# A fused linear attention and gated MLP on one core: more column groups of the first layer by the seven-product scheme, with v casts, sums and gates on GpSimd

## The chip, the core and the metric

The kernel runs on one core of one Trainium2 chip. The metric is device time in microseconds (us) of one execution, lower is better. Four compute engines matter here: TensorE (PE, with its weight loads shown apart as PEld), VectorE (DVE), ScalarE (ACT) and GpSimd (POOL). SyncE (SP) and GpSimd issue the DMAs. Each engine works off its own queue in order; semaphores tie the queues together.

## The reference

The inputs are q, k and v of 8 batches, 8 heads, 576 positions and 64 columns, and two weight matrices, 512 x 2048 and 2048 x 512. All are float32, and so is the output of 4608 x 512.

```python
q_p = concat(relu(q) * cos_w, relu(q) * sin_w)      # features, 128 wide
k_p = concat(relu(k) * cos_w, relu(k) * sin_w)
kv  = einsum('bhsf,bhsd->bhfd', k_p, v);  z = k_p.sum(axis=2)
x   = einsum('bhsf,bhfd->bhsd', q_p, kv) / (einsum('bhsf,bhf->bhs', q_p, z) + 1e-6)
h   = x.transpose(0, 2, 1, 3).reshape(4608, 512) @ w_in     # first layer
out = (h * cos(h)) @ w_out                                  # gate, second layer
```

## The kernel before

The 4608 tokens are cut into nine chunks of 512. Chunks 0 to 7 are the first 512 tokens of one batch each; chunk 8 collects the 64 left over of every batch. For each batch `attention` loads k, v and q by SP, makes the features with `prep` (ReLU times cosine or sine, float32 to float16, L419 on ACT or L420 on DVE, 128x512 each), casts v with `cast_v` (L433 ACT, L434 DVE), forms kv in `kv` (L446), transposes the q features by DMA in `q_dma` (L485) or on PE in `q_pe` (L475), and forms the numerator and denominator in `num` (L507 PE, L523 to L527 DVE). The normalised x is transposed on PE (`x_pe`, L547 and L551) for chunks up to 2 and by DMA (`x_dma`, L557) after that. Features of k and q lie in one tile `KQ`, with five slots of one token block each for k and five for q.

The first layer is in `layer1`. Chunks 0 and 1 run it on halves of the tokens (L604). From chunk 2 on, the 16 column tiles of h form four groups: group g holds tiles 2g and 2g+1 of the lower half and the same of the upper half. A group can be done in two ways.

- `layer1_plain` (L636): four banks, each four products of 128x512, 16 in all. Each bank then has a cosine on ACT (`gate`, L577) and a product on DVE (L579) that writes float16 into gT.
- `layer1_fast` (L740): the two by two block product by seven half-size products (Winograd's form), so 28 matmuls of 128x256. It needs four sums of weights (`w_in_sums`, L676) and four differences of x (`layer1_sums`, L697). Its products are gathered in three float32 tiles Y, U and Z by three copies on ACT (L748) and three additions on DVE (L752). Y gets a gate of its own (cosine L577, product L579), U and Z share a cosine of 1024 columns (L763) and a product of 1024 columns (L769), and the last part is gated straight out of PSUM.

Before, groups 0 and 1 of chunks 3 to 8 take the fast way, 12 groups; the others of chunks 2 to 8, 16 groups, the plain way. The sums of w_in cover two groups at once, 1024 columns each.

The second layer (`layer2`, L897) is by seven products from chunk 1 on, with sums of gT on DVE (L879, L924), copies on ACT (L908) and additions on DVE (L912). Stores of the output leave through POOL's queue (L803).

The order of the work is written out by a planner, `Plan`, when the kernel is built. Every step is added with an engine or a choice of engines, an occupation, a latency, a due time and the keys it reads and writes. `forward` simulates the engines with those costs, `run` repeats it over perturbed priorities (`ROUNDS`) and keeps the plan that ends first, and the instructions are then emitted in that order. Steps with `port=True` may not run on DVE and POOL at the same time in the plan. In the plan of before, POOL has no arithmetic beyond a few one-row casts that order DMAs (L970, L980, L995, L1002).

Of the kernel before, what the change touches and what calls it, by code (L numbers as in the profile page):

```python
# [17 lines left out]
class Plan:  # L18
# [11 lines left out]
    PASSES, ROUNDS = 12, 117  # L30
# [3 lines left out]
    BUSY = 2.2  # L34

# [6 lines left out]
    def add(self, eng, occ, lat, due, fn, rd=(), wr=(), dma=None, lane=None, late=0.0,  # L42
            lazy=None, port=False):
# [18 lines left out]
        for key in wr:  # L62
# [6 lines left out]
                               lazy=lazy, port=port))  # L69
# [40 lines left out]
    def forward(self, key):  # L110
# [14 lines left out]
        held, other = {"DVE": 0.0, "POOL": 0.0}, {"DVE": "POOL", "POOL": "DVE"}  # L125

        def shared(n, e):
            return st[n]["port"] and e in other

        def at(n, e):  # L130
            t = max(free[e], avail[n])
            return max(t, held[other[e]]) if shared(n, e) else t
# [5 lines left out]
        def first(n, e, t):  # L138
            opts = st[n]["opts"]
            return len(opts) == 1 or all(  # L140
                t + opts[e][1] <= max(free[x], avail[n]) + o[1] for x, o in opts.items())
# [12 lines left out]
        while todo:  # L154
# [44 lines left out]
            if shared(n, e):  # L199
                held[e] = free[e]  # L200
# [60 lines left out]
def kernel(  # L261
# [57 lines left out]
    KQ = sb("KQ", [P, 2, (NT + 1) * H * 2 * D])  # L319
    kp, qp = [KQ[:, n].rearrange("p (t h g d) -> p t h g d", t=NT + 1, h=H, g=2) for n in range(2)]  # L320
# [12 lines left out]
    G2.append(KQ[:, :, 0:JH * SM].rearrange("p h (j s) -> p h j s", j=JH))  # L333
# [21 lines left out]
    VCAST = ("DVE", "ACT")  # L355
# [3 lines left out]
    GATE1 = (w_in_sb[0:2, 0, Dff // 2 + 1:Dff // 2 + 2], [("w_in", 2)])  # L359
# [11 lines left out]
    def dve(occ, due, fn, rd, wr, lat=0.13, lazy=None, port=False):  # L371
        pl.add("DVE", occ, occ + lat, due, fn, rd, wr, lazy=lazy, port=port)
# [4 lines left out]
    def either(due, cost, fn, rd, wr):  # L377

        lat = {"DVE": 0.13, "ACT": 0.15, "POOL": 0.15}
        pl.add([(e, cost[e], cost[e] + lat[e], fn[e]) for e in cost], 0, 0, due, None, rd, wr, port=True)  # L380
# [29 lines left out]
    def prep(b, nm, t, g, eng, due, hs=slice(0, H), after=()):  # L410
        dst = (kp if nm == "k" else qp)
        out_, in_ = dst[:, t, hs, g, :], raw[nm][:, hs, t, :]
# [3 lines left out]
        wr = [(nm + "p", t, g, h) for h in heads]  # L416
# [7 lines left out]
    def cast_v(b, t, eng, due, hs=slice(0, H), nt=1):  # L424
# [7 lines left out]
        cost = {"DVE": 0.09 + 0.33 * f, "ACT": 0.12 + 0.5 * f, "POOL": 0.9}  # L432
# [36 lines left out]
    def q_pe(b, t, bank, key, eng, due):  # L469
# [3 lines left out]
        def mm():  # L473
            for h in range(H):
                nc.tensor.matmul(ps[:, h, :], lhsT=qp[:, t, h].rearrange("p g d -> p (g d)"),  # L475
                                 rhs=IDENT, is_transpose=True)
        pe(H, MMT, due, mm, [("qp", t, g, h) for g in range(2) for h in range(H)] + ["ID"], [key])
# [5 lines left out]
    def q_dma(b, t, due):  # L483
        dst, dkey = qdst(b, t)
        pl.add("SP", 1.25, 0, due, lambda: nc.sync.dma_start(  # L485
            out=dst, in_=qp[:, t].rearrange("p h g d -> p (h g d)"), transpose=True),
            [("qp", t, g, h) for g in range(2) for h in range(H)], [dkey],
# [76 lines left out]
    def mul(due, cost, fn, rd, wr, pool):  # L564

        if pool is None:
            dve(cost, due, lambda: fn(nc.vector), rd, wr)
        elif pool:
            pl.add("POOL", 3.4 * cost, 0.15 + 3.4 * cost, due, lambda: fn(nc.gpsimd), rd, wr,
                   port=True)  # L570
        else:
            dve(cost, due, lambda: fn(nc.vector), rd, wr, port=True)

    def gate(bank, key, dst, dkeys, due, pool=None, rd=()):
# [9 lines left out]
    def layer1(c):  # L584
# [3 lines left out]
        if c < 2:  # L588
            n = 0
            for quarter in range(4):  # L590
                for hf in range(2):
                    for jp in range(2):
# [15 lines left out]
                        pe(2 * NCT, MMH, due, mm, xk[2 * hf:2 * hf + 2] + [("w_in", quarter)],  # L608
# [21 lines left out]
    def layer1_plain(c, j, X, xk):  # L630
# [7 lines left out]
        pe(NCT, MM, due, mm, xk + [("w_in", j // 4)], [mk])  # L638
# [4 lines left out]
    FAST1 = {3: 2, 4: 2, 5: 2, 6: 2, 7: 2, 8: 2}  # L643
    SUMS_AT = min(FAST1) - 1
    Y_POOL, UZ_POOL = (), ()
    CH2, JF = NCT // 2, JH * P // 2


    WSA = {1: w_in_sb[:, 0:CH2, 2 * JF:3 * JF]}
    for n in (2, 3, 4):  # L650
        WSA[n] = sb(f"WS{n}", [P, CH2, JF])
    LATE = any(nf > 2 for nf in FAST1.values())

    def flat(t, dt=F16):
# [3 lines left out]
    WSB = {n: qT[n - 1].rearrange("p h s -> p (h s)").rearrange("p (c f) -> p c f", c=CH2)  # L658
           for n in range(1, 5)}
# [9 lines left out]
    def w_in_sums(f, due):  # L669
        W, JL = w_in_sb, JH * P  # L670
        lo, hi = slice(f * JF, (f + 1) * JF), slice(JL + f * JF, JL + (f + 1) * JF)
        a11, a12, a21, a22 = W[:, 0:CH2, lo], W[:, CH2:, lo], W[:, 0:CH2, hi], W[:, CH2:, hi]
        ws = WSB if f else WSA

        def tt(n, a, b, op, rd, wr):
            dve(0.61, due, lambda: nc.vector.tensor_tensor(out=ws[n], in0=a, in1=b, op=op),  # L676
                [("w_in", f), ("w_in", 2 + f)] + rd, wr + [("WS", n, f)] + ([("qT", n - 1)] if f else []), lazy=20.0, port=True)
        tt(3, a11, a21, ALU.subtract, [], [])
        tt(1, a21, a22, ALU.add, [], [] if f else [("w_in", 2)])
        tt(2, ws[1], a11, ALU.subtract, [("WS", 1, f)], [])  # L680
        tt(4, a12, ws[2], ALU.subtract, [("WS", 2, f)], [])
# [7 lines left out]
    def layer1_sums(c, X, xk):  # L689
# [6 lines left out]
        def tt(n, a, b, rd, wr=()):  # L696
            dve(0.33, start[c] - 1 + 0.3 * n, lambda: nc.vector.tensor_tensor(  # L697
                out=XS[n], in0=a, in1=b, op=ALU.subtract), xk + rd, [("XS", i, n)] + list(wr), port=True)
# [9 lines left out]
    def layer1_fast(c, g, X, xk):  # L708
# [14 lines left out]
        def lhs(n):  # L723
            if n > 0:
                return (lambda cc, j: (WSB if g // 2 else WSA)[n][:, cc, (2 * (g % 2) + j) * P:
# [373 lines left out]
    for c in range(2, NC):  # L1099
        if c < B:  # L1100
            attention(c)
        if c == SUMS_AT + 1:
            w_in_sums(0, start[c] - 12)
# [40 lines left out]
```

## Time and profile before

| what | value |
|---|---|
| device time, median of 3 runs | 285.42 us (284.47 to 286.86) |
| span of the profiled execution (its own time is given only as this span) | 282.8 us |
| PE busy | 272.4 us, 96% |
| PEld busy | 208.3 us, 74% |
| DVE busy | 247.5 us, 88% |
| ACT busy | 215.5 us, 76% |
| POOL busy | 26.0 us, 9% |
| plain groups, L636: 256 matmuls of 128x512, mean of one | 379 ns |
| fast groups, L740: matmuls of 128x256, mean of one | 272 to 273 ns |
| product of a gate, L579 on DVE, 128x512, mean of one | 683 ns |
| cosine of a gate, L577 on ACT, 128x512, mean of one | 595 ns |
| product of U and Z, L769 on DVE, 128x1024, mean of one | 1217 ns |

A mean is the time from start to end of one instruction. Instructions of one engine overlap at their edges, so a row of equal ones advances faster than its mean: eight matmuls of 128x512 advance by 1.73 us, and gates on DVE by 0.60 us each. The groups of the page give the busy time, the mean of one instruction, and the idle time of the engine ahead of it. The chain of work is followed back from the last instruction to whatever released each step.

### The profile page before, as it was taken

What the parts mean: (1) busy time and instruction counts of PE and PEld (TensorE: products, weight loads), DVE (VectorE), ACT (ScalarE), POOL (GpSimd) and SP (SyncE); (2) the same over time, 40 slices, a digit from 0 to 9 for tenths busy, and PEclk for the clock granted to TensorE, in tenths of its full rate; (3) what the DMA queues carried; (4) which work ended last, traced back from release to release, by engine and by line L of the source; (5) the groups of instructions that cost most, each with busy time, mean ns of one, the idle gap of its engine ahead of it and who ended that gap; (6) DMA issues with size and microseconds to landing.
All of it is one profiled execution on the core that took longest, in us unless ns stands there. A gap on an engine that the chain in (4) does not pass through costs nothing.

```text
span 282.8 us, 6578 instructions
## 1 busy us (share of the span) xinstructions
PE 272.4 (96%) x2619; PEld 208.3 (74%) x2619; DVE 247.5 (88%) x458; ACT 215.5 (76%) x367; POOL 26.0 (9%) x53
## 2 busy tenths in 40 slices
PE   7889989999999999999999999999999999999993
PEld 2468856669866688777877887787777877876882
DVE  2986878999999999999999999999899999967941
ACT  2947897999999999999999999995834666456420
POOL 1412020011000020002000200020002001100200
PEclk9999999999999999999999999999999999999999
DMA  6999999799989999999997899786024001100124
GB/s 214 303 204 273 258 310 300 251 270 212 344 222 240 228 227 362 170 245 224 254 268 186 265 290 224 164 159 167 2 56 168 21 2 75 76 2 0 68 82 150
DMA packets 77567, 53.30 MB, mean 188 GB/s; under 512 B 46048, under 2 KB 75232, under 8 KB 77536
## 3 DMA queue, kind: packets, MB, share of 16 engines
q1 hardware_dynamic: 70032, 39.73, 55.7%
q0 software_dynamic: 6784, 12.59, 17.1%
q10 hardware_dynamic: 720, 0.57, 0.6%
q8 instruction: 20, 0.33, 0.5%
q14 instruction: 11, 0.09, 0.1%
HBM read 36.74 MB, written 9.44 MB: 163 GB/s over the span
## 4 chain that ended last, share of the span: by engine, by line
PE 84%; DMA 8%; ACT 3%; DVE 2%; issue 1%; SPq 0%; ACTq 0%; DVEq 0%
PE M L897 33%; PE M L636 16%; PE M L740 8%; PE M L604 8%; PE TR L740 4%; PE M L834 4%; DMA vm<-in_v_dram 4%; PE TR L636 3%; PE ATT L507 3%; DMA qT<-KQ 3%; PE ATT L446 3%; DMA qm<-in_q_dram 2%; ACT KQ L419 1%; PE M L475 1%; DVE x L527 1%
## 5 line engine op out<-in xcount | busy, mean ns | idle before, releaser
L577 ACT ACTIVATE ch<-M 128x512 f32<-128x512 f32 x90 | 52.8, 595 | 11.1 <-PE M L604 4.1
L897 PEld LDWEIGHTS <-gT 128*128 128x128 f16 x560 | 53.7, 98 | 9.3
L579 DVE TENSOR_TENSOR gT<-M,ch 128x512 f16<-128x512 f32 x83 | 55.4, 683 | 4.7 <-ACT ch L577 4.2
L897 PE MATMUL M<-w_out_sb,gT 128*128 128x256 f16 x448 | 54.9, 273 | 0.0
L636 PE MATMUL M<-xT,w_in_sb 128*128 128x512 f16 x184 | 45.9, 379 | 0.0
L419 ACT ACTIVATE KQ<-qm,CS 128x512 f16<-128x512 f32 x59 | 40.1, 718 | 4.5 <-DMA qm<-in_q_dram 4.5
L419 ACT ACTIVATE KQ<-km,CS 128x512 f16<-128x512 f32 x56 | 38.3, 719 | 0.0
L636 PEld LDWEIGHTS <-w_in_sb 128*128 128x128 f16 x256 | 24.4, 98 | 18.3
L803 POOL DMA_DIRECT2D out_dram<-ost x32 | 17.0, 537 | 213.9 <-DVE ost L912 134.8
L897 PE MATMUL M<-T,S 128*128 128x256 f16 x256 | 32.5, 273 | 0.0
L604 PE MATMUL M<-xT,w_in_sb 128*128 128x256 f16 x256 | 30.6, 273 | 0.1
L897 PEld LDWEIGHTS <-S 128*128 128x128 f16 x256 | 24.9, 98 | 4.0
L604 PEld LDWEIGHTS <-w_in_sb 128*128 128x128 f16 x256 | 24.5, 98 | 3.9 <-issue 0.3
L908 ACT ACTIVATE ost<-M 128x512 f32<-128x512 f32 x31 | 18.5, 597 | 10.2 <-PE M L897 10.1
L527 DVE TENSOR_TENSOR x<-ATT,rec 128x512 f16<-128x512 f32 x32 | 22.1, 691 | 1.1
L740 PEld LDWEIGHTS <-w_in_sb 128*128 128x128 f16 x192 | 18.5, 98 | 4.9 <-issue 0.2
L912 DVE TENSOR_TENSOR ost<-M,ost 128x512 f32<-128x512 f32 x24 | 16.4, 681 | 4.0 <-issue 3.5
L507 PEld LDWEIGHTS <-qT 128*128 128x128 f16 x320 | 15.1, 98 | 4.7 <-issue 0.5
L752 DVE TENSOR_TENSOR Z<-M,Z 128x512 f32<-128x512 f32 x23 | 15.6, 684 | 2.3 <-PE M L740 1.9
L879 DVE TENSOR_TENSOR S<-gT 128x2048 f16<-128x2048 f16 (+1 forms) x16 | 17.3, 1085 | 0.2
L748 ACT ACTIVATE Z<-M 128x512 f32<-128x512 f32 x19 | 11.3, 596 | 6.6 <-PE M L740 6.4
L740 PEld LDWEIGHTS <-WS 128*128 128x128 f16 x144 | 13.6, 98 | 3.3 <-issue 0.2
(130 smaller groups left out, 421.8 us busy)
## 6 DMA issues: line engine op xcount, KB each, us to landing
out_dram<-ost POOLq DMA_DIRECT2D x32, 256.0 KB, 4.3
qm<-in_q_dram SPq DMA_DIRECT2D x8, 640.0 KB, 5.8
km<-in_k_dram SPq DMA_DIRECT2D x8, 640.0 KB, 7.8
qm<-in_q_dram SPq DMA_DIRECT2D x8, 512.0 KB, 5.6
km<-in_k_dram SPq DMA_DIRECT2D x8, 512.0 KB, 6.7
vm<-in_v_dram SPq DMA_DIRECT2D x6, 640.0 KB, 6.4
vm<-in_v_dram SPq DMA_DIRECT2D x6, 512.0 KB, 5.9
w_in_sb<-in_moe_w_in_dram POOLq DMA_DIRECT2D x4, 512.0 KB, 8.9
```

The costliest lines, as they stand in the source:

```text
L419: fn = {"ACT": lambda: nc.scalar.activation(out=out_, in_=in_, func=AF.Relu, scale=sc), "DVE": lambda: nc.vector.tensor_scalar(out=out_, i ...
L507: nc.tensor.matmul(bank[hb][:, hh * D1:(hh + 1) * D1], lhsT=a[:, h, :], rhs=z[:, h, :], start=(i == 0), stop=(i == len(parts) - 1))
L527: nc.vector.tensor_tensor(out=split(x16[n][:, hs, :], k), in0=A[:, :, :, 0:D], in1=split(rec[n][:, hs], k).unsqueeze(3).broadcast_to((P, k ...
L577: act(0.5, due, lambda: nc.scalar.activation(out=ch[c], in_=bank, func=AF.Sin, bias=math.pi / 2.0, scale=1.0), [key], [("ch", c)])
L579: mul(due, 0.61, lambda q: q.tensor_tensor(out=dst, in0=bank if len(dst.shape) == 2 else bank.rearrange("p (j s) -> p j s", j=dst.shape[1] ...
L604: nc.tensor.matmul(M1[m][:, jj * 2 * P:(jj + 1) * 2 * P], lhsT=w_in_sb[:, cc, j * P:(j + 1) * P], rhs=X[:, cc, ts], start=(cc == 0), stop= ...
L636: nc.tensor.matmul(M, lhsT=w_in_sb[:, cc, j * P:(j + 1) * P], rhs=X[:, cc, :], start=(cc == 0), stop=(cc == NCT - 1))
L740: nc.tensor.matmul(bank[0][:, j * TH:(j + 1) * TH], lhsT=a(cc, j), rhs=b[:, cc, :], start=(first and j == 0 and cc == 0), stop=(last and j ...
L803: pl.add(eng, 0.9 if eng == "POOL" else 0.65, 0, due, lambda: q.dma_start(out=dst, in_=src_), keys, [], dma=(nb, 355.0))
L879: dve(0.07 + 1.07 / NG, due, lambda: nc.vector.tensor_tensor(out=out_[:, sl], in0=a[:, sl], in1=b[:, sl], op=op), rd, wr, port=True)
L897: nc.tensor.matmul(bank[0][:, tt * MH:(tt + 1) * MH], lhsT=a[:, j, tt * P:(tt + 1) * P], rhs=b[:, j, :], start=(first and tt == 0 and j == 0),
L908: act(0.5, due, lambda: nc.scalar.activation(out=dst, in_=view(bank), func=AF.Copy), [bank[1]], dk)
```

## The change

- `FAST1` sends 2 groups of chunk 2, 3 groups of chunks 3 to 6 and 4 groups of chunks 7 and 8 through the seven products, 22 groups in place of 12.
- The sums of w_in are made per group (512 columns), each when the first chunk needs it; group 3 writes into tiles of qT that are free by then. The keys of w_in are finer to match.
- v casts from chunk 2 on go to POOL (`VCAST`). The gate of Y goes to POOL (`Y_ON`). The product of U and Z and the differences of x may go to DVE or POOL as the planner finds (`UZ_ON`, `XS_ON`); in the plan that comes out 4 of 22 and 21 of 28 go to POOL.
- The planner's exclusion of DVE and POOL (`port`) is gone, POOL's costs are lower, a small preference for POOL is added, and `ROUNDS` is 200.
- q features have three slots in `KQ` in place of five.

```diff
-    PASSES, ROUNDS = 12, 117
+    PASSES, ROUNDS = 12, 200
+    RATHER = {"POOL": -0.5}
...
-            return max(t, held[other[e]]) if shared(n, e) else t
+            return max(free[e], avail[n])
...
-                t + opts[e][1] <= max(free[x], avail[n]) + o[1] for x, o in opts.items())
+                t + opts[e][1] + self.RATHER.get(e, 0.0)
+                <= at(n, x) + o[1] + self.RATHER.get(x, 0.0) + 1e-9 for x, o in opts.items())
...
-    KQ = sb("KQ", [P, 2, (NT + 1) * H * 2 * D])
-    kp, qp = [KQ[:, n].rearrange("p (t h g d) -> p t h g d", t=NT + 1, h=H, g=2) for n in range(2)]
+    NQ = 3
+    KQ = sb("KQ", [P, (NT + 1 + NQ) * H * 2 * D])
+    KQ6 = KQ.rearrange("p (t h g d) -> p t h g d", t=NT + 1 + NQ, h=H, g=2)
+    kp, qp = KQ6[:, 0:NT + 1], KQ6[:, NT + 1:]
...
-    VCAST = ("DVE", "ACT")
+    VCAST = ("POOL",)
...
-        out_, in_ = dst[:, t, hs, g, :], raw[nm][:, hs, t, :]
+        slot = t if nm == "k" else t % NQ
+        out_, in_ = dst[:, slot, hs, g, :], raw[nm][:, hs, t, :]
...
-        cost = {"DVE": 0.09 + 0.33 * f, "ACT": 0.12 + 0.5 * f, "POOL": 0.9}
+        cost = {"DVE": 0.09 + 0.33 * f, "ACT": 0.12 + 0.5 * f, "POOL": 0.2 + 0.45 * f}
...
-    def mul(due, cost, fn, rd, wr, pool):
-        if pool is None:
-            dve(cost, due, lambda: fn(nc.vector), rd, wr)
-        elif pool:
-            pl.add("POOL", 3.4 * cost, 0.15 + 3.4 * cost, due, lambda: fn(nc.gpsimd), rd, wr,
-                   port=True)
-        else:
-            dve(cost, due, lambda: fn(nc.vector), rd, wr, port=True)
+    def mul(due, cost, fn, rd, wr, on=""):
+        slow = 2.15 * cost
+        opts = {"DVE": ("DVE", cost, cost + 0.13, lambda: fn(nc.vector)),
+                "POOL": ("POOL", slow, slow + 0.15, lambda: fn(nc.gpsimd))}
+        pl.add([opts[e] for e in ("DVE", "POOL") if e[0] in (on or "D")], 0, 0, due, None, rd, wr)
...
-    FAST1 = {3: 2, 4: 2, 5: 2, 6: 2, 7: 2, 8: 2}
-    SUMS_AT = min(FAST1) - 1
-    Y_POOL, UZ_POOL = (), ()
-    CH2, JF = NCT // 2, JH * P // 2
+    FAST1 = {2: 2, 3: 3, 4: 3, 5: 3, 6: 3, 7: 4, 8: 4}
+    SUMS_AT = {g: min(c for c, n in FAST1.items() if n > g) for g in range(max(FAST1.values()))}
+    LATE_G = (3,)
+    Y_ON, UZ_ON, XS_ON = [dict.fromkeys(range(2, NC), e) for e in ("P", "DP", "DP")]
+    CH2, JF = NCT // 2, 2 * P
...
-            dve(0.33, start[c] - 1 + 0.3 * n, lambda: nc.vector.tensor_tensor(
-                out=XS[n], in0=a, in1=b, op=ALU.subtract), xk + rd, [("XS", i, n)] + list(wr), port=True)
+            mul(start[c] - 1 + 0.3 * n, 0.36, lambda q: q.tensor_tensor(
+                out=XS[n], in0=a, in1=b, op=ALU.subtract), xk + rd, [("XS", i, n)] + list(wr),
+                XS_ON.get(c))
...
-                c in UZ_POOL)
+                UZ_ON.get(c))
...
-        out(Y, zk[0], 0, 0, d, c in Y_POOL)
+        out(Y, zk[0], 0, 0, d, Y_ON.get(c, ""))
...
-        if c == SUMS_AT + 1:
-            w_in_sums(0, start[c] - 12)
-        if c == B - 1 and LATE:
-            w_in_sums(1, start[c] - 6)
+        for g, at in SUMS_AT.items():
+            if c == at:
+                w_in_sums(g, start[c] - (6 if g in LATE_G else 12))
```

## The prediction, made before the changed kernel ran

> **What bounds the kernel now.** I read the page's busy time and slices first, then the engines' busy time by stage, then the chain of work, then single rows.
>
> ```profile
> span 282.8 us, 6578 instructions
> ...
> PE 272.4 (96%) x2619; PEld 208.3 (74%) x2619; DVE 247.5 (88%) x458; ACT 215.5 (76%) x367; POOL 26.0 (9%) x53
> ...
> PE   7889989999999999999999999999999999999993
> ...
> DVE  2986878999999999999999999999899999967941
> ACT  2947897999999999999999999995834666456420
> POOL 1412020011000020002000200020002001100200
> ```
>
> The same as a table by stage (columns: length; then busy us and instructions of PE, PEld, DVE, ACT, POOL; granted clock; DMA share; GB/s):
>
> ```profile
> 50.00:80.00 30.00, 29.87 (x333) 23.59 (x331) 28.80 (x55) 27.67 (x48) 2.21 (x4) 1.00 0.96 273
> 80.00:190.00 110.00, 109.89 (x1085) 84.04 (x1083) 105.84 (x188) 106.73 (x183) 8.02 (x16) 1.00 0.96 231
> 190.00:250.00 60.00, 60.00 (x515) 47.16 (x513) 55.54 (x94) 33.33 (x56) 4.67 (x9) 1.00 0.26 69
> ```
>
> From 50 us on TensorE never stops, at full granted clock. But DVE is idle only 4.2 us of the 110 from 80 to 190 and 4.5 us of the 60 after that, and ACT only 3.3 us of the 110. POOL is the only free engine. So the kernel is bound by TensorE with DVE right behind it: 8.7 us of DVE idle is all there is to spend between 80 and 250 us.
>
> The chain of work gives TensorE's pace (start, length, what):
>
> ```profile
> 84.81 1.73 PE M L636 x8
> ...
> 109.04 7.67 DMA qT<-KQ
> ...
> 134.39 0.87 PE M L740 x8
> ```
>
> Eight matmuls of 512 columns advance by 1.73 us, eight of 256 by 0.87. The q transposes stand on the chain once.
>
> DVE's pace, from its timeline (start, length, then an engine, line, tile and shape):
>
> ```profile
> 118.27 1.22 DVE L769 TENSOR_TENSOR gT<-Z,ch 128x1024 f16<-128x1024 f32 x1
> 119.40 0.68 DVE L579 TENSOR_TENSOR gT<-M,ch 128x512 f16<-128x512 f32 x1
> 120.00 0.68 DVE L912 TENSOR_TENSOR ost<-M,ost 128x512 f32<-128x512 f32 x1
> ```
>
> Start to start, a product of 1024 costs 1.13 us and a product or addition of 512 costs 0.60.
>
> Last, what happens when POOL and DVE touch SBUF at once. POOL's timeline, then DVE's over the same moment:
>
> ```profile
> 23.76 0.19 POOL L980 COPY w_out_sb<-w_in_sb 1x4 f16<-1x4 f16 x1 [6.16 <-DMA w_in_sb<-in_moe_w_in_dram]
> ...
> 35.14 0.53 POOL L1002 CAST w_out_sb<-qm 1x2 f16<-1x2 f32 x1 [9.24 <-DMA qm<-in_q_dram]
> ```
>
> ```profile
> 34.35 1.27 DVE L420 TENSOR_SCALAR KQ<-km,CS 128x512 f16<-128x512 f32 x3
> ```
>
> A cast of two elements takes 0.19 us beside a gate out of PSUM, and 0.53 beside the last of three feature instructions, ending 0.05 us after it (34.35 + 1.27 = 35.62 against 35.67). POOL stood still for a whole DVE instruction. This pair excludes each other.
>
> **The change, part by part.** The profiled span of 282.8 lies 2.6 under the median of 285.42; I keep that 2.6 as constant and sum against the span.
>
> *TensorE.* Plain group: 16 x 1.73/8 = 3.46 us. Fast group: 28 x 0.87/8 = 3.05, or 3.06 by the less rounded rows. Ten more fast groups (two each in chunks 2, 7 and 8, one each in 3 to 6) remove 10 x 0.40 = 4.0 us, all on the path.
>
> *DVE, counted in the built program's order, at start-to-start prices.* Gates out of PSUM -30 x 0.60 = -18.0; Y gates that go to POOL -12 x 0.60 = -7.2; additions into Y, U, Z +30 x 0.60 = +18.0; products of U and Z +6 x 1.13 = +6.8; weight sums +16 x 0.34 - 4 x 0.60 = +3.0; differences of x -17 x 0.34 = -5.8; features +9 x 0.39 = +3.5; v casts -3.0. Sum -2.7. Since TensorE's time falls by 4.0, DVE's idle time between 80 and 250 becomes 8.7 + 2.7 - 4.0 = 7.4 us.
>
> *ACT.* Cosines out of PSUM -30 x 0.48, copies +30 x 0.48, cosines of Y +10 x 0.48, of U and Z +10 x 0.95, features -9 x 0.61, v casts -9.6. Sum -0.8: nothing, hidden while ACT stays under TensorE.
>
> *POOL* gains 12 casts of 1024 and 6 of 512, 21 differences, 22 Y gates and 4 products of U and Z. No row has such an operation. Below, DVE's own durations (0.69, 0.42, 0.42, 0.68, 1.22) give 40 us. Above, POOL's memset of 128x512 takes 0.52 us for one stream, so three streams (two in, one out) take 1.57 and the sum is 111. I take two streams, 1.05 us per 512 products and per 1024 cast, nearest to the memset: 12 x 1.05 + 6 x 0.52 + 21 x 1.05 + 22 x 1.05 + 4 x 2.1 = 69 us, 36% of the 190 us from 75 to 265. POOL has room; it is not the bound.
>
> *The collision.* In that stretch the new order has 79 DVE instructions with both inputs in SBUF (sums of gT, U and Z products, weight sums, differences) and 22 features. If an instruction that finds POOL at work waits for it, it waits half of some 1.1 us: 101 x 0.36 x 0.55 = 20 us. If only the features collide, 22 x 0.36 x 0.55 = 4.4 us. Nothing excludes 0. The trace shows total exclusion where it shows any, so I take 15, nearer the upper end. That is 15 - 7.4 = 7.6 us more than DVE's idle time hides, and it is on the path: behind a held DVE instruction stand gates out of PSUM, and TensorE waits for their banks.
>
> [...]
>
> *First use.* The built order has a library reload on POOL ahead of its first product, the differences of chunk 2. The last v cast of chunk 3 would end near 77.0 (casts now begin at 74.4, plus 2.6 on POOL), the last piece of x for chunk 2 comes at 79.0, so 2.0 us are hidden. No row shows a reload. Nearest is ACT's table load, 1.28 us: nothing. Farthest is a 512 KB weight load landing in 8.9 us: 6.9. I take 0; cover is the wait for x.
>
> [...]
>
> *q features in three slots.* The fourth feature pair must wait until the first transpose has landed, 5.1 us after issue, plus two features of 0.61: issue at 6.3 us against 3.75 today, 2.6 us later per batch. Six batches, 0 to 15 us; I take 0, because TensorE waited 0.4 us in all at L507 and transposes run a chunk ahead. The cover goes if DVE falls behind.
>
> *POOL's queue.* 28 stores (0.54 us each) now stand between products, and a product behind a store waits for that store's addition on DVE. The plan spaces them; late DVE makes them late. Priced within the collision. SP issues the same DMAs. The first 75 us lose only the finer keys and get a new plan: 0, within 1 either way.
>
> *Sum:* 285.4 - 4.0 + 7.6 = 289.0 us.
>
> **The rivals.**
> - *The saving pays (faster).* DVE and POOL run side by side and only the features collide: 4.4 is under 7.4, so 281.4, and to 284 with a reload partly seen. For it: no row shows a two-input DVE instruction held. Against it: 7.4 us of idle time in 170 is thin. It ends above 285.4 from the point where stalls pass 7.4 + 4.0 = 11.4 us.
> - *They cancel (same).* Stalls of 9 to 14 us, or the reload uncovered with stalls small: 283 to 288.
> - *The full lock.* Both ends block, and the two-input sums wait each time: 20 us, 294.
> - *Transposes.* q features late by 2.6 us a batch on the path: 281.4 + 15 = 296 at most; the first sign is TensorE waiting in L507.
>
> **How the numbers follow.** About 1% is what a measurement can tell from no change here (the three runs span 0.8%): faster is under 282.6, slower over 288.3. Collision over the idle time, full lock included: 0.48, of which 0.43 ends above 288.3 and 0.05 below. The saving pays: 0.29, of which 0.23 is under 282.6. They cancel: 0.21, all within 1%. Transposes: 0.02, slower. So faster 0.23, same 0.32, slower 0.45. The likeliest is the collision, 289.0, its own range 286 to 294. The range reaches down to the saving with a little less TensorE waiting and up to the full lock: 281.0 to 294.5.
>
> **What would show it.** TensorE's L740 and L636 rows must give 4.0 us less advance. Right: L879, L769 and L420 rows on DVE longer than 1.22, 1.22 and 0.48 in the mean, with the surplus near 15 us, TensorE gaps released by DVE or ACT between 80 and 190, POOL busy for 60 to 90 us. Wrong: those rows unchanged and TensorE without gaps, then the time is near 281.4. A gap of some us on POOL ahead of L697 and on TensorE near 80 us shows the reload. Rows of POOL near 2 us and Y gates late on the path would make POOL the bound, which I did not price.

## The result, and the profile after

The changed kernel takes 315.25 us (313.54 to 316.00, four runs), the kernel before 285.31 beside it (284.47 to 286.86): a ratio of 1.103, 95% interval 1.098 to 1.108. It is 30 us slower, and 26 us above the forecast of 289.0.

The page of the changed kernel, the same lines as before: busy time, then the slices of TensorE, DVE, ACT and POOL.

```profile
span 311.6 us, 6967 instructions
...
PE 275.6 (88%) x2739; PEld 221.5 (71%) x2739; DVE 280.6 (90%) x450; ACT 215.8 (69%) x366; POOL 113.2 (36%) x118
...
PE   6889989998799958799779979987998979799993
...
DVE  2968989998999999999999999999999999788962
ACT  2947987779589944699669959985656555466620
POOL 1402200612830375459232643483045256612210
```

TensorE's unbroken row of nines is gone: from a quarter of the way on there are sevens, and later fives. DVE has kept its nines and grown from 247.5 to 280.6 us busy, with fewer instructions (450 against 458). By stage (length; busy us and instructions of PE, PEld, DVE, ACT, POOL; clock; DMA share; GB/s):

```profile
80.00:190.00 110.00, 95.89 (x983) 76.67 (x981) 108.26 (x157) 84.52 (x145) 50.92 (x45) 0.98 0.89 206
190.00:250.00 60.00, 55.79 (x561) 47.01 (x560) 57.71 (x87) 42.55 (x73) 25.00 (x24) 1.00 0.49 110
```

Between 80 and 190 us DVE is idle for 1.74 of 110 us while TensorE is idle for 14. The bound has moved from TensorE to DVE. Which of DVE's rows grew, from the groups (busy us, mean ns, then idle time ahead). The first two lines are of the kernel before, where the sum of gT stands at L879 and the feature at L420:

```profile
L879 DVE TENSOR_TENSOR S<-gT 128x2048 f16<-128x2048 f16 x12 | 14.6, 1218 | 0.1
L420 DVE TENSOR_SCALAR KQ<-qm,CS 128x512 f16<-128x512 f32 x21 | 9.3, 480 | 4.9 <-DMA qm<-in_q_dram 4.9
```

```profile
L577 DVE TENSOR_TENSOR gT<-M,ch 128x512 f16<-128x512 f32 x61 | 41.0, 684 | 3.6 <-ACT ch L575 2.9
...
L878 DVE TENSOR_TENSOR S<-gT 128x2048 f16<-128x2048 f16 x12 | 22.3, 1859 | 0.3
...
L422 DVE TENSOR_SCALAR KQ<-qm,CS 128x512 f16<-128x512 f32 x32 | 20.7, 680 | 4.8 <-DMA qm<-in_q_dram 4.8
...
L768 DVE TENSOR_TENSOR gT<-Z,ch 128x1024 f16<-128x1024 f32 x12 | 19.6, 1635 | 0.3 <-ACT ch L762 0.3
...
L675 DVE TENSOR_TENSOR w_in_sb<-w_in_sb 128x512 f16<-128x512 f16 x4 | 4.9, 1236 | 0.0
```

The gate out of PSUM takes 684 ns, as before (683). What reads both inputs from SBUF grew: sums of gT from 1218 to 1859 ns, products of U and Z from 1217 to 1635, sums of w_in to 1236 (415 in the kernel below that has the fast groups only). The features grew from 480 to 680. I call a row's time above its own time in the kernel before its surplus. All DVE surplus together is 37.8 us; DVE's own work without it is 242.8 us, against 246.7 before. And what TensorE waited for:

```profile
PE M L896 <- DVE S L878: 5.7, 3, 4.2
PE ATT L509 <- DVE x L529: 3.6, 3, 1.8
PE M L739 <- DVE Z L751: 3.5, 4, 1.7
PE M L739 <- DVE qm L751: 2.0, 1, 2.0
PE M L739 <- POOL XS L697: 2.0, 1, 2.0
```

Four of the five longest waits are for DVE. TensorE's gaps above its own pace, added up after 50 us, are 32.5 us against 0.8 before. So the span closes: 282.8 - 4.0 (groups) + 31.7 (gaps) + 1.1 (busy time of TensorE that is missing in the first 50 us: 43.62 against 44.74) = 311.6.

Not all of the gaps are waits. In two stretches of 3.4 us the granted clock is 0.50 (the third number from the end), with TensorE busy all through; the kernel before has none until its matmuls are done:

```profile
118.14:121.55 3.41, 3.41 (x28) 2.55 (x25) 3.34 (x6) 1.03 (x2) 3.39 (x4) 0.50 0.51 103
268.32:271.74 3.42, 3.42 (x19) 2.44 (x17) 2.07 (x3) 2.38 (x4) 1.80 (x2) 0.50 0.38 149
```

The matmuls of 128x256 advance by 0.213 us each there in place of 0.109, which makes 3.3 of the 32.5 us. Each stretch begins within 1 us of the end of a wait of TensorE (4.16 us up to 117.79, 2.00 us up to 267.41). No run tries whether the wait is the cause, and another wait of 1.99 us, at 82.5, is not followed by one.

One place tells how a single DVE instruction can lose 4.5 us. DVE first, then POOL, then TensorE over the same moment:

```profile
108.09 0.68 DVE L577 TENSOR_TENSOR gT<-M,ch 128x512 f16<-128x512 f32 x1
108.68 5.77 DVE L878 TENSOR_TENSOR S<-gT 128x2048 f16<-128x2048 f16 x1
```

```profile
108.47 0.55 POOL L802 DMA_DIRECT2D out_dram<-ost  x1 [1.09 <-DVE ost L911]
109.02 1.07 POOL L437 CAST V<-vm 128x1024 f16<-128x1024 f32 x1
110.03 1.16 POOL L697 TENSOR_TENSOR XS<-xT 128x512 f16<-128x512 f16 x1
111.13 1.05 POOL L437 CAST V<-vm 128x1024 f16<-128x1024 f32 x1
112.14 1.15 POOL L697 TENSOR_TENSOR XS<-xT,XS 128x512 f16<-128x512 f16 x1
113.24 1.68 POOL L437 CAST V<-vm 128x512 f16<-128x512 f32 x1
```

```profile
117.79 1.58 PE L896 MATMUL M<-T,S 128*128 128x256 f16 x8 [4.16 <-DVE S L878]
```

The sum begins at 108.68, while POOL issues a store, and ends at 114.45, in the last of the five POOL instructions behind that store. POOL's first four run at their undisturbed time; DVE gets nothing until they are through, and then the fifth waits for DVE (1.68 us in place of 0.60). TensorE's wait of 4.16 us is for a later sum of the same group, which DVE ends at 117.73.

### The profile page after: what moved, and what is told of

Its sections match the earlier page's. It is cut to its first block, busy times and chain, and to the rows that moved or that the text cites. A ratio compares the mean times of both kernels' runs of the same rounds, so it can differ in the third digit from the quotient of the medians.

```text
span 311.6 us, 6967 instructions
## 1 busy us (share of the span) xinstructions
PE 275.6 (88%) x2739; PEld 221.5 (71%) x2739; DVE 280.6 (90%) x450; ACT 215.8 (69%) x366; POOL 113.2 (36%) x118
## 4 chain that ended last, share of the span: by engine, by line
DVE 45%; PE 33%; DMA 7%; issue 6%; ACT 3%; POOL 3%; SPq 1%; DVEq 0%; ACTq 0%
PE M L896 13%; DVE S L878 6%; DVE Z L751 6%; DVE gT L768 5%; PE M L739 5%; DVE gT L577 5%; PE M L602 5%; DVE KQ L422 5%; DMA qT<-KQ 4%; DVE x L529 3%; DMA vm<-in_v_dram 3%; PE TR L739 2%; DVE gT L923 2%; POOL XS L697 2%; PE M L634 2%
## 5 line engine op out<-in xcount | busy, mean ns | idle before, releaser
L575 ACT ACTIVATE ch<-M 128x512 f32<-128x512 f32 x63 | 37.2, 596 | 13.2 <-PE M L602 5.9
L739 PEld LDWEIGHTS <-w_in_sb 128*128 128x128 f16 x352 | 34.1, 99 | 17.2 <-issue 11.7
L577 DVE TENSOR_TENSOR gT<-M,ch 128x512 f16<-128x512 f32 x61 | 41.0, 684 | 3.6 <-ACT ch L575 2.9
L577 POOL TENSOR_TENSOR gT<-Z,ch 128x512 f16<-128x512 f32 x15 | 20.5, 1366 | 57.4 <-ACT ch L575 57.3
L437 POOL CAST V<-vm 128x1024 f16<-128x1024 f32 (+1 forms) x18 | 20.0, 1136 | 34.2 <-DMA vm<-in_v_dram 25.7
L739 PEld LDWEIGHTS <-WS 128*128 128x128 f16 x240 | 23.5, 99 | 8.5 <-issue 3.9
L751 DVE TENSOR_TENSOR Z<-M,Z 128x512 f32<-128x512 f32 x41 | 27.4, 681 | 1.0 <-PE M L739 0.9
L602 PEld LDWEIGHTS <-w_in_sb 128*128 128x128 f16 x256 | 24.5, 98 | 4.6 <-issue 1.5
L878 DVE TENSOR_TENSOR S<-gT 128x2048 f16<-128x2048 f16 (+1 forms) x16 | 25.5, 1596 | 0.5
L747 ACT ACTIVATE Z<-M 128x512 f32<-128x512 f32 x34 | 19.9, 596 | 8.6 <-PE M L739 7.9
L422 DVE TENSOR_SCALAR KQ<-qm,CS 128x512 f16<-128x512 f32 x32 | 20.7, 680 | 4.8 <-DMA qm<-in_q_dram 4.8
L762 ACT ACTIVATE ch<-Z 128x1024 f32<-128x1024 f32 x16 | 16.9, 1057 | 11.4 <-DVE Z L751 11.4
L529 DVE TENSOR_TENSOR x<-ATT,rec 128x512 f16<-128x512 f32 x32 | 22.1, 692 | 1.1
```

Source lines behind the costliest of these rows:

```text
L422: "DVE": lambda: nc.vector.tensor_scalar(out=out_, in0=in_, scalar1=0.0, scalar2=sc, op0=ALU.max, op1=ALU.mult)}
L437: "POOL": lambda: nc.gpsimd.tensor_copy(out=out_, in_=in_)}
L529: nc.vector.tensor_tensor(out=split(x16[n][:, hs, :], k), in0=A[:, :, :, 0:D], in1=split(rec[n][:, hs], k).unsqueeze(3).broadcast_to((P, k ...
L575: act(0.5, due, lambda: nc.scalar.activation(out=ch[c], in_=bank, func=AF.Sin, bias=math.pi / 2.0, scale=1.0), [key], [("ch", c)])
L577: mul(due, 0.61, lambda q: q.tensor_tensor(out=dst, in0=bank if len(dst.shape) == 2 else bank.rearrange("p (j s) -> p j s", j=dst.shape[1] ...
L602: nc.tensor.matmul(M1[m][:, jj * 2 * P:(jj + 1) * 2 * P], lhsT=w_in_sb[:, cc, j * P:(j + 1) * P], rhs=X[:, cc, ts], start=(cc == 0), stop= ...
```

## The experiments

The theory after the result: POOL's reads of SBUF and DVE's two-input and feature instructions shut each other out, and with DVE full every loss becomes a gap on TensorE. Rivals: POOL's results come late; the fast groups themselves overload DVE and ACT; three q slots; the planner's new order as such.

The table gathers what the expectations are held against. Own and surplus are DVE's, POOL is its arithmetic after 50 us, gaps are TensorE's after 50 us, all in us from the profiled run; the time is the median.

| kernel | time | 95% interval of the ratio | own | surplus | POOL | gaps |
|---|---|---|---|---|---|---|
| before | 285.3 | 1 | 246.7 | 0.8 | 0 | 0.8 |
| change | 315.3 | 1.098 to 1.108 | 242.8 | 37.8 | 88.3 | 32.5 |
| POOL only | 298.9 | 1.034 to 1.051 | 238.1 | 19.8 | 63.3 | 13.9 |
| POOL writes | 286.0 | 0.999 to 1.004 | 244.0 | 3.6 | 92.6 | 4.8 |
| fast groups only | 291.7 | 1.014 to 1.028 | 263.1 | 0.5 | 0 | 11.2 |
| planned apart | 297.2 | 1.031 to 1.045 | 246.7 | 16.5 | 70.8 | 16.7 |
| planned free | 296.1 | 1.027 to 1.043 | 256.3 | 8.4 | 32.6 | 16.3 |
| slots only | 287.3 | 1.002 to 1.011 | 248.7 | 0.7 | 0 | 2.7 |
| five slots | 289.5 | 1.008 to 1.020 | 247.3 | 1.0 | 0 | 5.6 |
| casts only | 291.4 | 1.013 to 1.025 | 247.5 | 4.4 | 16.7 | 8.3 |
| U, Z and differences on DVE | 291.2 | 1.016 to 1.022 | 250.0 | 13.8 | 50.3 | 11.5 |
| differences on DVE | 295.5 | 1.025 to 1.039 | 248.3 | 14.9 | 55.5 | 14.8 |
| stores on SP | 302.0 | 1.053 to 1.061 | 243.0 | 25.5 | 90.3 | 19.8 |
| U, Z, differences on DVE, stores on SP | 289.7 | 1.009 to 1.017 | 249.4 | 10.5 | 51.7 | 8.4 |
| before, stores on SP | 284.0 | 0.993 to 0.997 | 246.6 | 1.0 | 0 | 0.2 |

**POOL's work alone, with the twelve fast groups of before.**

```diff
-    FAST1 = {2: 2, 3: 3, 4: 3, 5: 3, 6: 3, 7: 4, 8: 4}
+    FAST1 = {3: 2, 4: 2, 5: 2, 6: 2, 7: 2, 8: 2}
```

> The changed kernel with the 12 fast groups of before: POOL has the v casts, 12 Y gates, most differences and U-Z products, and TensorE the old work. Theory A: the two-input DVE rows and the features are stretched as in the changed kernel, in proportion to POOL's time; some 20 to 25 us are lost, of which the work taken off DVE (about 14 us) and the 8.7 us of idle time pay part: 287 to 300 us. Rival B: the fast groups are at fault, so with the old ones it is 280 to 286.

Measured: 298.89 us. Taking 8.6 us of own work off DVE (246.7 to 238.1) and handing it to POOL put 19.8 us of surplus on it, and the kernel lost 13.5 us. So the move to POOL loses by itself, with no more fast groups.

**The change, with POOL writing but not reading.** Each product, difference and cast on POOL reads one column and then fills its output with memsets; the values of those outputs are left out. Plan, order and semaphores stay those of the change.

```diff
...
+        def tensor_tensor(out, in0, in1, op):
+            c = WRITER.corner
+            nc.gpsimd.tensor_tensor(out=c(out), in0=c(in0), in1=c(in1), op=op)
+            for i in range(2):
+                nc.gpsimd.memset(out, 0.01)
...
-                "POOL": ("POOL", slow, slow + 0.15, lambda: fn(nc.gpsimd))}
+                "POOL": ("POOL", slow, slow + 0.15, lambda: fn(WRITER))}
```

> The changed kernel in the same plan, but each product or cast on POOL reads one column only (so it waits as before) and then fills its output with memsets of about the same length: the values of the v casts, Y gates, differences and U-Z products on POOL are left out. Theory A with the read side as what is shared: sums of gT and U-Z products on DVE go back to about 1.22 us, features stay stretched, time 284 to 294 us. If the write side is shared by all: rows stay stretched and the time stays over 305. Rival B (plan, chains, slots): the time stays at 310 to 316 though the rows are short.

Measured: 286.04 us with POOL as busy as in the change (92.6 us against 88.3). DVE's groups:

```profile
L439 DVE TENSOR_SCALAR KQ<-qm,CS 128x512 f16<-128x512 f32 x32 | 16.6, 552 | 5.8 <-DMA qm<-in_q_dram 5.8
...
L895 DVE TENSOR_TENSOR S<-gT 128x2048 f16<-128x2048 f16 x12 | 14.6, 1220 | 0.3
L785 DVE TENSOR_TENSOR gT<-Z,ch 128x1024 f16<-128x1024 f32 x12 | 14.6, 1218 | 0.3 <-ACT ch L779 0.3
```

The two-input rows are back at their own 1220 and 1218 ns; only the features keep a little (552 against 480), 3.1 of the 3.6 us surplus. This is the run that decides: same plan, same waits on POOL, same occupation of POOL, and 29 us of the 30 are gone with the reads. POOL's lateness is left in it, and is worth 3.6 us of TensorE's waits in all:

```profile
PE M L756 <- POOL XS L389: 3.6, 3, 1.6
```

It also shows what the prediction's 281.4 was worth: with nearly no collision the time is 286.0, not 281.4, since the gaps are still 4.0 us above those of before.

**The pair by itself.** A kernel that computes no part of the reference runs rows of DVE instructions alone and then beside rows of POOL instructions.

> No part of the computation: trains of DVE and POOL instructions of the change's shapes, alone and side by side, in stages that start together. Theory A: the stage of six sums of 2048 (1.14 us each start to start) beside six POOL products of 512 lasts about the sum of both alone, not the longer one; the same for 1024-wide U-Z products and for features; gates out of PSUM (0.60) stay unchanged beside POOL. Beside memsets on POOL, which only write, sums and U-Z products stay unchanged and features lengthen. If a DVE instruction waits once for the POOL instruction in flight, each DVE instruction of a stage is longer by at most one POOL instruction (1.3 us); if POOL wins again and again, the first DVE instruction takes the whole train (7 us or more). Rival B: no row changes by over 10%.

DVE's timeline (start, length of the whole row, line: L49 two-input sum, L52 feature, L58 gate out of PSUM; the last number counts instructions). The first three are alone, the next three beside POOL products, then a sum beside POOL casts, a sum and features beside POOL memsets:

```profile
22.38 4.99 DVE L49 TENSOR_TENSOR S<-A,B 128x2048 f16<-128x2048 f16 x4
...
32.20 4.14 DVE L52 TENSOR_SCALAR K<-F,SC 128x512 f16<-128x512 f32 x8
36.26 2.86 DVE L58 TENSOR_TENSOR GA<-M,G 128x512 f16<-128x512 f32 x4
...
39.09 12.36 DVE L49 TENSOR_TENSOR S<-A,B 128x2048 f16<-128x2048 f16 x6
...
66.53 11.64 DVE L52 TENSOR_SCALAR K<-F,SC 128x512 f16<-128x512 f32 x12
...
78.14 8.66 DVE L58 TENSOR_TENSOR GA<-M,G 128x512 f16<-128x512 f32 x12
...
86.78 11.22 DVE L49 TENSOR_TENSOR S<-A,B 128x2048 f16<-128x2048 f16 x6
...
121.73 7.51 DVE L49 TENSOR_TENSOR S<-A,B 128x2048 f16<-128x2048 f16 x6
...
137.05 10.14 DVE L52 TENSOR_SCALAR K<-F,SC 128x512 f16<-128x512 f32 x12
```

A sum goes from 1.25 us each (4.99/4) to 2.06 (12.36/6) beside products and 1.87 beside casts, and stays at 1.25 beside memsets. Single sums in the contended rows last 2.17 us, 0.95 more than the 1.22 alone: with both engines running rows without a break, they take turns, one instruction each, and a DVE instruction loses 0.95 us, three quarters of a POOL product of 1.26, not half of one. POOL's product goes from 1.26 to 2.12 us. A feature is held off in the same way (1.37 in the contended part, 0.48 alone), by memsets too (1.13). The gate out of PSUM does not notice (0.72 each, start to start, in both rows).

So a sum waits beside POOL work that reads SBUF (2.17 us beside products) and not beside POOL work that only writes it (1.23 us beside memsets). The kernel whose POOL writes says the same: its sums take 1220 ns, against 1859 in the change, where POOL reads as well.

**The fast groups alone**, nothing on POOL:

```diff
-    VCAST = ("POOL",)
+    VCAST = ("DVE", "ACT")
...
-    Y_ON, UZ_ON, XS_ON = [dict.fromkeys(range(2, NC), e) for e in ("P", "DP", "DP")]
+    Y_ON, UZ_ON, XS_ON = [dict.fromkeys(range(2, NC), e) for e in ("D", "D", "D")]
```

> The change's 22 fast groups with no arithmetic on POOL (v casts on DVE or ACT; Y gates, differences and U-Z products on DVE). Theory A, DVE and POOL shut each other out: every two-input DVE row back at its old mean (sums of gT 1.22 us, features 0.48), but DVE carries some 25 us more than before against 8.7 us of idle time, so 293 to 303 us, under the 315.3 of the change. Rival B, the longer chains of the fast groups and the three q slots stall TensorE whatever POOL does: 310 or more.

Measured: 291.70 us, somewhat under what was expected. There is no surplus (0.5 us), but DVE's own work is 263.1 us, 16.4 more than before. By stage:

```profile
80.00:190.00 110.00, 107.46 (x1124) 88.03 (x1122) 107.87 (x194) 108.33 (x187) 6.68 (x13) 1.00 0.96 223
```

DVE and ACT are both full, and TensorE has lost 2.5 us in this stretch alone. Ten more fast groups take 4.0 us off TensorE and put 16.4 on DVE, which had 8.7 to spare there; POOL was to carry that, and POOL's help costs more than it carries. The two halves of the change cost 6 and 14 us alone and 30 together.

**A planner that knows of the collision.** The plan forbids DVE's two-input work, its features and POOL's arithmetic to overlap, with POOL's measured durations.

```diff
-            return max(free[e], avail[n])
+            t = max(free[e], avail[n])
+            return max(t, held[other[e]]) if shared(n, e) else t
...
-        slow = 2.15 * cost
+        slow = 1.18 if cost < 0.4 else 2.15 * cost
```

> The change with the planner told to keep every two-input or feature instruction of DVE apart from POOL's arithmetic, with POOL's measured durations (product of 512 1.3 us, difference 1.18). v casts and Y gates stay on POOL; 12 of 28 differences do. Theory A: the stretched rows shrink, DVE's surplus falls from 35 us to under 15, and so does TensorE's waiting: 288 to 300 us. Theory C, the drift between plan and chip undoes any such plan: surplus and time as in the change, over 305.

> As the planned-apart kernel, but the planner may also give v casts to DVE or ACT and Y gates to DVE, and the differences stay on DVE. POOL keeps 14 or so casts and some 10 products. Theory A: the surplus is under 8 us and TensorE has 4.0 us less to do, 283 to 292 us. Theory C: over 295.

The first, with casts and Y gates held on POOL, took 297.19 us, within its 288 to 300, with 16.5 us of surplus, above the 15 expected; the second, which may place every one of these freely (differences on DVE), 296.10, above its expected 283 to 292. The plans keep the engines apart on paper; on the chip they meet all the same. In the second that is not all: its surplus is 8.4 us and DVE's own work is 9.6 us up. That the queues drift against the plan's costs is my reading, not tried by itself.

**Slots and plan.** Twelve fast groups, nothing on POOL, three q slots; and the same with five.

```diff
-    NQ = 3
+    NQ = 5
...
```

> The changed kernel with the 12 fast groups of before and nothing on POOL, so that three q slots, sums of w_in in quarters and the planner without its exclusion are all that is left of the change. Theory A: these cost nothing, 283 to 288 us. Rival B in part (the three slots make q features late): 290 or more, with TensorE waiting in the numerator's matmuls for q transposes.

> The slots kernel (12 fast groups, nothing on POOL, 287.3 us) with five q slots in place of three. If the slots cost its 1.7 us, 285 to 286 us and no gap of over 1 us in the numerator's matmuls; if it was the new plan, 287 again.

287.32 and 289.46 us. Three slots are not slower than five, so the slots cost nothing that shows; what is left, 2 to 4 us, I put down to a plan made anew. Differences of 2 us between kernels with different plans are therefore not read below.

**Casts alone on POOL**, twelve fast groups: 18 casts, 16.7 us of POOL.

```diff
-    FAST1 = {2: 2, 3: 3, 4: 3, 5: 3, 6: 3, 7: 4, 8: 4}
+    FAST1 = {3: 2, 4: 2, 5: 2, 6: 2, 7: 2, 8: 2}
...
-    Y_ON, UZ_ON, XS_ON = [dict.fromkeys(range(2, NC), e) for e in ("P", "DP", "DP")]
+    Y_ON, UZ_ON, XS_ON = [dict.fromkeys(range(2, NC), e) for e in ("D", "D", "D")]
```

> The 12 fast groups of before, everything on DVE and ACT but the v casts, which are on POOL: 16 us of POOL arithmetic in trains of three. DVE's surplus 4 to 9 us against 3 us of its own work saved and 9.6 of ACT's: 285 to 292 us. Under 284 would mean that ACT's relief is worth more than the collisions.

291.41 us, with a surplus of only 4.4. That is more than the surplus explains; TensorE's longest wait is for ACT's copies of Z, 2.8 us in three waits, so part of it may be the plan.

**Which POOL work does the harm?** First only the differences go back to DVE, then the products of U and Z as well:

```diff
-    Y_ON, UZ_ON, XS_ON = [dict.fromkeys(range(2, NC), e) for e in ("P", "DP", "DP")]
+    Y_ON, UZ_ON, XS_ON = [dict.fromkeys(range(2, NC), e) for e in ("P", "DP", "D")]
...
+    Y_ON, UZ_ON, XS_ON = [dict.fromkeys(range(2, NC), e) for e in ("P", "D", "D")]
```

> The change with only the differences of x moved to DVE; the U-Z products may still go to POOL and 2 do. POOL keeps casts, Y gates and these. If the differences carry the loss, as they take part in most of the long waits and TensorE waits for them directly: 291 to 296 us and a surplus of 14 to 18 us. If each us of POOL's time costs the same: 25 of 88 us gone, surplus 27 us, 302 to 307.

> The change with the differences of x and the U-Z products on DVE, so that POOL keeps the v casts and the 22 Y gates, some 45 us in place of 78, and stands less often in a train. Theory T: DVE's surplus falls by more than POOL's time does, to under 15 us of the 37.8; against that DVE has 12 us more of its own: 291 to 300 us. Rival, each meeting costs the same: surplus 21 us, 300 to 306 us.

Both came out as expected: 295.47 us with 14.9 of surplus, and 291.23 with 13.8. Taking 21 differences off POOL (and with them, by the new plan, two of the four products of U and Z) removes 23 of the 37.8 us of surplus and 20 us of time. After 50 us DVE is then held 21 times, 0.67 us each, in place of 41 times. The differences are short, but they come in rows of two to four, and casts and gates stand beside them in longer rows.

**Do rows of POOL work hold DVE off?** A kernel that computes no part of the reference sets one DVE instruction against a row of POOL instructions with outputs of their own.

> No part of the computation: trains of POOL products and DVE instructions as in the first stages kernel, but each instruction of a train has its own output, so that nothing waits inside a train. Theory T, a train of POOL products without waits between them never gives the port up: a single sum of 2048 or a single feature instruction of DVE that meets the start of a train of six is longer by nearly the whole train, 6 us or more. Rival, they alternate as they do when each waits for the one before: longer by at most 1.3 us. The other way round, a train of six sums on DVE should hold one POOL product off for up to 7 us if T holds for DVE too, or 1.2 if not.

The theory of the held row fell: a sum met by six POOL products took 2.03 us, and a POOL product met by six sums took 2.25 us in place of 1.26, the wait for one sum. Without more, turns are taken one for one. The next kernel used the change's own shapes, and in its last parts put a store ahead of the row:

```python
def pD():
    nc.gpsimd.dma_start(out=out[0:P, :], in_=O)
```

> No part of the computation: POOL trains of the change's own shapes (v casts into the strided V1 layout, float16 differences with and without a chain, the two mixed, and products mixed with differences) against one sum of 2048 or one feature instruction of DVE between gates. In the changed kernel 14.8 us of DVE's 36.8 us were lost over more than one POOL instruction. Theory M, mixed trains do not let DVE in between two of their instructions: the single DVE instruction is longer by 2 us or more beside mixed or cast trains, by at most 1.3 beside trains of products. Theory S, it is the store issued on POOL just ahead: over 2 us in the stages with a store alone. Theory N, neither: at most 1.3 us everywhere.

Without a store, sums took up to 2.18 us and features up to 1.38; in one part each DVE came first and POOL waited (1.22 and 0.48). With one store just ahead of the row (DVE, then POOL):

```profile
132.66 6.72 DVE L55 TENSOR_TENSOR SS<-A,B 128x2048 f16<-128x2048 f16 x1
...
140.62 6.16 DVE L58 TENSOR_SCALAR KS<-F,SC 128x512 f16<-128x512 f32 x1
```

```profile
132.33 0.72 POOL L80 DMA_DIRECT2D out_dram<-O  x1
133.05 1.07 POOL L68 CAST V<-VM 128x1024 f16<-128x1024 f32 x1
134.06 1.16 POOL L72 TENSOR_TENSOR XS<-X 128x512 f16<-128x512 f16 x1
135.16 1.06 POOL L68 CAST V<-VM 128x1024 f16<-128x1024 f32 x1
136.16 1.15 POOL L72 TENSOR_TENSOR XS<-X 128x512 f16<-128x512 f16 x1
137.25 1.04 POOL L68 CAST V<-VM 128x1024 f16<-128x1024 f32 x1
```

The DVE instruction that begins while POOL issues the store is held off for the whole row behind it: the sum loses 5.5 us, the feature 5.7 (over five differences). It is the picture of 108.68 us in the changed kernel, made on purpose. The kernel with POOL's work alone has it too: at 192.03 us a feature begins in a store and takes 3.87 us, over three differences. But it is no rule without exception. In all runs with such POOL work, 11 sums, products, differences or features of DVE after 50 us began in a store and had over 0.15 us to go when the POOL arithmetic right behind it began. Nine of them were held; two sums of the kernel planned apart were not, here one:

```profile
112.94 1.21 DVE L885 TENSOR_TENSOR S<-gT 128x2048 f16<-128x2048 f16 x1
```

There POOL's difference waited (1.90 us in place of 1.15). What tells the two cases apart is not known.

**The stores moved to SP**, in the change, in the kernel with U, Z and differences on DVE, and in the kernel before:

```diff
-            put(due, five[:, 2 * h:2 * h + 2, :], blocks(O, n), keys, nc.gpsimd, "POOL")
+            put(due, five[:, 2 * h:2 * h + 2, :], blocks(O, n), keys)
...
```

> The change with the stores of the chunks before the last issued by SP instead of POOL, nothing else. Theory S (a DVE instruction that begins while POOL issues a store is held off for the whole row of POOL instructions behind that store): the 14.8 us that the changed kernel loses in DVE instructions lying over two or more POOL instructions nearly vanish (under 4), the DVE surplus falls from 37.8 to 18-26 us, and the time falls to 299-308 us. Rival (the long holds come from rows of POOL work as such): surplus stays 33-40 and the time at 311-318. A third outcome, SP's transposes and loads held up behind its waiting stores, would show as TensorE gaps released by DMA with the surplus reduced all the same.

> The change with differences and U-Z products on DVE (as in the kernel so named) and the stores on SP. Its long holds were already gone with the stores on POOL (12.9 of 13.8 us of surplus lay over one POOL instruction), so by theory S moving the stores changes little: surplus 12-15 us, 289-293 us. The rival, that any store on POOL costs DVE something by itself, would give surplus under 10 and 285-289.

> The kernel before with the same stores on SP: prices that edit by itself. Without arithmetic on POOL there is nothing behind a store that could hold DVE, so by theory S no gain: 285 to 290 us, any loss being transposes and loads that stand behind a waiting store on SP's queue. If stores on POOL cost DVE by themselves it would come out under 284.

In the change: 302.01 us, 13 less, surplus 25.5, as the store theory expected. DVE's groups:

```profile
L768 DVE TENSOR_TENSOR gT<-Z,ch 128x1024 f16<-128x1024 f32 x14 | 19.5, 1394 | 0.5 <-ACT ch L762 0.5
L878 DVE TENSOR_TENSOR S<-gT 128x2048 f16<-128x2048 f16 x12 | 18.3, 1523 | 0.3
L422 DVE TENSOR_SCALAR KQ<-qm,CS 128x512 f16<-128x512 f32 x30 | 17.5, 617 | 5.1 <-DMA qm<-in_q_dram 4.9
```

The changed kernel has six DVE instructions that lose over 1.5 us, 14.7 us in all; here there is none, and the longest single loss under two POOL instructions is 0.96. One number missed: the loss lying over two POOL instructions (those that it overlaps by 0.3 us or more) is 8.3 us where under 4 was expected, in small pieces. And the store does not explain all that went. Of the six long holds two began in a store or as it ended (4.55 and 2.26 us, 6.8 together); the other four met a product of U and Z on POOL, 2.35 us long by itself, and the new plan has three such products that lose DVE 0.9 us in all. So some 7 of the 12 us of surplus that went are the stores', and most of the rest is where the new plan put U and Z.

With U, Z and differences on DVE, the stores make little (289.71 against 291.23) as expected, with a surplus of 10.5 a little under the 12 to 15. In the kernel before, 283.99 against 285.49, a ratio of 0.995 (0.993 to 0.997): 1.5 us faster where no gain was expected, and a hair under the 284 below which the rival was to hold, that a store on POOL costs something by itself. It is the one version here that beats both kernels. The cause of that 1.5 us stays open: DVE has no surplus there to lose, and the plan is a new one.

## Why the prediction was wrong

- *The collision, 15 us, was the step that failed.* In place and kind it was right: two-input work and features were held, gates out of PSUM were not, and the time went through DVE to TensorE. Its share of hits was right too: 41 of 113 contending instructions after 50 us lose over 0.1 us, 0.36. Its price was not. The sum had one price for every hit, half of some 1.1 us, 0.55; the loss is 36.8 us over 41 hits, 0.90 each. The ordinary hit was nearly priced right: 35 of the 41 lose 22.1 us, 0.63 each, and the kernels without a hold of over 1.6 us agree (0.68 over 19 hits with U, Z and differences on DVE, 0.72 over 35 with the stores on SP). The other six lose 14.7 us, which the sum had no term for: four met one of POOL's products of U and Z, 2.35 us long and priced like the rest, and lose 1.73 to 2.20; two began in a store or as it ended, with a row of POOL work behind it, and lose 4.55 and 2.26. So 113 x 0.36 x 0.90 = 37 in place of 20, and I had then gone under my own 20 to 15.
- *From the surplus to the time*: this step held. A surplus of 37.8 less the 7.4 of idle time is 30.4, and TensorE's gaps grew by 31.7, of which 3.3 are the stretches at half clock.
- *The full lock, 20 us, was no upper bound.* It took for granted that DVE waits for one POOL instruction and for half of it. The trace of before had one hold, of a tiny cast by the last feature (the 0.19 beside it is a copy of four elements, not a cast; casts of two take 0.18), with POOL as the one that waits. It shows that they exclude each other, and not for how long DVE can be held. Nothing bounded the price from above, and the range should have been drawn from a whole instruction or more per hit.
- *The idle time as a cushion, 7.4 us*: DVE's idle time between 80 and 250 us fell from 8.7 to 4.0 us, so about what could be used was used. But it does not come where the stall is: with 3.6 us of surplus, under the cushion, the kernel whose POOL only writes still had 4.0 us more of gaps.
- *TensorE, -4.0*: right, by the sum of the span above. The first 50 us cost 1.1 where I had 0 within 1.
- *DVE's own work, -2.7*: measured 242.8 - 246.7 = -3.9. Right, and it hid the main thing: without POOL it is +16.4.
- *POOL, 69 us*: at its undisturbed times (casts 1.05 and 0.60, differences 1.15, Y gates 1.26, U and Z 2.35) the same work is 77.5, stretched 88.3 by DVE. Between the bounds, a little low.
- *First use, 0*: right. In the kernel of the pair by itself POOL goes from its copy straight into its first product, with two MODIFY_POOL_CONFIG (at 8.06 and 8.09), which I take to be the reload, between them:

```profile
7.94 0.19 POOL L74 COPY MP<-MD 128x1 f32<-128x1 f32 x1 [5.37 <-DVE MD L73]
8.15 5.29 POOL L61 TENSOR_TENSOR PY<-PF,PG 128x512 f16<-128x512 f32 x4
```

  The gap is 0.02 us. In the change the same two stand ahead of POOL's first difference (at 78.79 and 78.82), and POOL waited 1.27 us there, for x. So no wait for a reload shows in either.
- *q slots, 0*: nothing against it, 287.3 against 289.5 with five, as far as plans that differ by 2 us can tell.
- *POOL's queue, priced within the collision*: this was the part that I passed over. I had 28 stores standing between products and saw only that a product may wait for a store. A store ahead of a row of products can be worse for DVE than the products (4.55 us against 0.63 for an ordinary hit).
- *Rivals*: the full lock named the mechanism, and the runs ended 21 us above its 294 (281.4 + 20 - 7.4). The others did not happen.

## What to carry to other kernels

Ask of an engine that stands idle what it shares with the full one. Moving two-input SBUF work to POOL took 20 us of work off DVE (263.1 to 242.8) and put 37.8 us of waiting on it. A usual hit cost 0.6 to 0.7 us here, half of a POOL instruction or a little more, but the sum goes by the long ones: bound a collision from above with a whole instruction of the other engine per hit, its longest one included, and where that engine also issues DMAs, with the whole row that may follow one. A pair that is seen to exclude each other once says nothing about how long. And when an edit takes 4 us off the bound, look first at what it adds to the engine right behind: here 16.4 us on an engine with 8.7 to spare.

## What the runs showed of the hardware

- DVE and POOL take turns, one instruction each, when both run rows of work that collides: a sum takes 2.17 us in place of 1.22, POOL's product 2.12 in place of 1.26.
- A store issued by POOL can break the turns: a DVE instruction that began while it was issued waited for the row of POOL instructions behind (6.72 us in place of 1.22, 6.16 in place of 0.48, five instructions each), in 9 of the 11 places that the traces have. What in the store does it is open.
- POOL's memsets leave two-input DVE work alone (1.23 us) and still hold features (1.13 in place of 0.48).
- TensorE's granted clock was 0.50 for 3.4 us twice in the changed kernel, each time within 1 us of a wait of TensorE (4.16 and 2.00 us); after another of 1.99 us it was not.
